# Second-layer sums in two alternating pairs of banks whose idle pair serves attention in fixed steps, and zero products on both row groups

## The chip, the core and the metric

The kernel runs on one core of one Trainium2 chip. The metric is the device time of one execution in microseconds; the time before is 2119.36 us, the median of three runs (2116.33 to 2122.65). Engines are named as in the profile: PE (TensorE matmul), PEld (its weight loads), DVE (VectorE), ACT (ScalarE), POOL (GpSimd) and SP (SyncE, which here issues all DMAs).

## The reference

Agent attention over 4 batches of 12480 tokens with 128 features and 49 agents, then a two-layer network with a squared ReLU, all in fp32:

```python
a2k = sm(agents, k)            # softmax over the 12480 keys, scale 1/sqrt(128)
agent_v = a2k @ v              # 49 x 128 per batch
q2a = sm(q, agents)            # softmax over the 49 agents
x = q2a @ agent_v              # 49920 tokens x 128
h = x @ w_in                   # 128 -> 2048
r = np.maximum(h, 0.0)
out = (r * r) @ w_out          # 2048 -> 128
```

So the work of a batch has an order: all its scores of k, their maximum, the sums over v, and only then can the first layer of its tokens start.

## The kernel before

The 49920 tokens are 52 groups of 960 (13 per batch). For each group, `q_scores` (L291) makes the scores against the agents on PE; `q_shift` (L303, DVE) takes the maximum off; exponent, sum, division and a split into a high and a low fp32r half follow on ACT, DVE and POOL; `q_transpose` (L329, PE) turns the result round, `q_copy` (L337, ACT) brings it to SBUF, and `q_spread` copies it to the other row group by two DMAs. The product `agent_v @ w_in` is folded into one 49 x 2048 matrix per batch (`w_make`, L268), again as high and low halves, so that the first layer is a product with K = 49.

The main loop has 832 steps: group s has 16, i is the step. A step runs `mm1` (L353, six products into one pair of PSUM banks `h`, two row groups side by side), `relu` (L365) and `square` (L369) on ACT, `high` (L373) and `low` (L377) on DVE, and `mm2` (L379, twelve products) for the step that lies LAG = 4 before. Eight steps of `mm2` (j = 0 to 7) add up one output tile of 480 tokens in two banks `out0` and `out1`, one for each row group. `store` (L389) then copies one bank on ACT (L392), adds the other on DVE (L393) and issues the DMA. `mm2` with j = 0 of the next tile starts in the same two banks (L383, L387).

PSUM has eight banks: four for two buffers of `h`, two for `out`, two for `ps_att`, the one pair that serves all attention work in the loop (`bank`, L149). Before the loop, `bank` also hands out `h` buffers.

While the loop runs through one batch, the next batch's attention is woven in: 13 pieces of k (`k_scores`, `k_copy`, `k_pmax`), the maximum over all (`k_max`), 13 pieces of v (`v_hi`, `v_lo`, `k_sub`, `k_exp`, `k_hi`, `k_lo`, `v_acc` L219, `v_sum` L236), `a_final` (L243) and four `w_make`. The order on every engine is written out: each piece of work is put at a time in steps with `at`, and all are sorted by it. `chain` (L412) finds the times: an engine takes at most one piece of attention work per step, a table `hop` gives the least distance from engine to engine, and a range of steps in `banks` keeps a second product out of `ps_att` until the first one's reader has had its step. The products may lie in any step. Work within a step comes as mm1 (i), relu (i + .1), mm2 (i + .2), attention (i + .5), square (.55), high (.6), low (.65).

Before the loop, in the opening, the first batch's attention runs alone: 13 pieces of k scores with one zero product each (`warm_up`, L484: a 64-row product of zeros into `out1`, whose result nobody reads), the maximum, 13 pieces of v (`v_acc_whole`, L227, into `out0`), the weights' conversion from the words as they come (`win_make`, `wo_make` on DVE, L100 to L106), `a_final`, and half of `w_make`. Pieces 0 to 2 of the second batch's k (AHEAD = 3) are scored there too.

Of the kernel before, what the change touches and what calls it, by code (L numbers as in the profile page):

```python
# [9 lines left out]
F32 = mybir.dt.float32  # L10
# [15 lines left out]
def agent_attention_relu2_kernel(ctx: ExitStack, tc: tile.TileContext, qT, kT, v, agT, w_in, w_out, outT):  # L26
# [25 lines left out]
    ew = ctx.enter_context(tc.tile_pool(name="ew", bufs=4))  # L52
    ps_h = ctx.enter_context(tc.tile_pool(name="ps_h", bufs=2, space=bass.MemoryType.PSUM))
    ps_o = ctx.enter_context(tc.tile_pool(name="ps_o", bufs=1, space=bass.MemoryType.PSUM))
    ps_a = ctx.enter_context(tc.tile_pool(name="ps_a", bufs=1, space=bass.MemoryType.PSUM))

    ag_sb = cpool.tile([P, B, 2, A], F32, name="ag_sb")
    nc.sync.dma_start(out=ag_sb, in_=agT)
# [84 lines left out]

    kts, vts, pes, pss = {}, {}, {}, {}

    many = [True]
    turn = [0]

    def bank():  # L149
        turn[0] += 1  # L150
        if many[0] and turn[0] % 3:
            return ps_h.tile([P, 2, 512], F32, name="h")
        return ps_a.tile([P, 2, 512], F32, name="ps_att")

    def piece(n):
        return sk[:, n * G:(n + 1) * G, :]
# [86 lines left out]
    def a_final(step, b):  # L243

        if step == 0:
            if b:
                nc.vector.tensor_tensor(acc[:, 0], acc[:, 0], acc[:, 1], op=ALU.add)
            nc.vector.tensor_tensor(acc[:, 0, :C], acc[:, 0, :C], acc[:, 0, C + 2:], op=ALU.add)
        elif step == 1:
            ps = pss["a"] = bank()[:, 0]  # L250
            nc.tensor.transpose(ps[:, :A2], acc[:, 0, :C], ident[:A2, :A2])
            nc.tensor.matmul(ps[:, P:P + A2], acc[:, 0, C:C + 1].to_broadcast([A2, P]), ident[:A2, :A2], start=True, stop=True)
        elif step == 2:
            t = pss.pop("a")[:, :2 * P].rearrange("p (t x) -> p t x", x=P)
            nc.vector.tensor_copy(av, t[:, :, :A])
            nc.vector.scalar_tensor_tensor(out=av[:, 1], in0=t[:, 1, A:A2], scalar=1e-9, in1=av[:, 1], op0=ALU.add, op1=ALU.add)
            nc.vector.tensor_tensor(av[:, 0], t[:, 0, A:A2], av[:, 0], op=ALU.add)
        else:
            nc.vector.reciprocal(av[:, 1], av[:, 1])
            nc.vector.tensor_tensor(a2[:, :, :A], av[:, 0:1].to_broadcast([P, 2, A]), av[:, 1:2].to_broadcast([P, 2, A]), op=ALU.mult)  # L260

# [3 lines left out]

    W = {}

    def w_make(b, f, step):  # L268
        if f == 0 and step == 0:
            W[b] = (wk.tile([P, NJ, P], F32R, name="w_hi"), wk.tile([P, NJ, P], F32R, name="w_lo"))  # L270
        wh, wl = W[b]
        js = slice(2 * f, 2 * f + 2)
        if step == 0:
            pss["w", f] = bank()[:, 0]
            nc.tensor.matmul(pss["w", f][:AW, :], a2.rearrange("p t a -> p (t a)")[:, :AW], win_sb[:, f * 512:(f + 1) * 512], start=True, stop=True)  # L275
        else:
            ps = pss["w", f].rearrange("p (j e c) -> p j e c", e=2, c=P)
            for e in range(2):
                if step == 1:
                    nc.scalar.copy(wh[ra[e], js], ps[ra[e], :, e])  # L280
                else:
                    nc.vector.tensor_tensor(wl[ra[e], js], ps[ra[e], :, e], wh[ra[e], js].bitcast(F32), op=ALU.subtract)  # L282
# [96 lines left out]
    def mm2(i):  # L379
        t, j = divmod(i, NJ)  # L380
        gh, gl = ghs.pop(i), gls.pop(i)
        if j == 0:
            outs[t] = [ps_o.tile([P, 512], F32, name=f"out{u}") for u in range(2)]  # L383
        todo = [(w, gh, e) for e in range(2) for w in (wo_hi, wo_lo)] + [(wo_hi, gl, e) for e in range(2)]
        for x, (w, g, e) in enumerate(todo):
            for u in range(2):
                nc.tensor.matmul(outs[t][u][:, :TT], w[rg[u], 2 * j + e, :], g[rg[u], e, :], start=j == 0 and x == 0, stop=j == NJ - 1 and x == 5)  # L387
# [7 lines left out]


    LAG = 4
    AHEAD = 3
    steps = []

    def at(t, f, *args):
# [4 lines left out]
    hop = {"PE": {"PE": 1, "ACT": 1, "DVE": 1}, "ACT": {"PE": 2, "ACT": 1, "DVE": 0, "POOL": 0, "SP": 0},  # L406
           "DVE": {"PE": 2, "ACT": 1, "DVE": 1, "POOL": 1, "SP": 0}, "POOL": {"PE": 3, "ACT": 2, "DVE": 2, "POOL": 1}}
    ends = {i for i in range(NG + LAG) if i >= LAG and (i - LAG) % NJ == NJ - 1}
    taken = {(e, i) for i in ends for e in ("ACT", "DVE")}
    banks = set()  # L410

    def chain(t, todo):  # L412

        first = prev = None
        while todo:
            n = 1
            while todo[0][0] == "PE" and n < len(todo) and todo[n][1] in reads_bank and todo[n][0] != "PE":
                n += 1  # L420
            t += hop[prev][todo[0][0]] if prev else 0
            while True:
                g, p, ts = t, None, []
                for e, *_ in todo[:n]:
                    g += hop[p][e] if p else 0
                    while (e, g) in taken:
                        g += 1
                    ts.append(g)
                    p = e
                held = range(ts[0], ts[-1] + 1) if todo[0][0] == "PE" else ()  # L430
                if not banks.intersection(held):
                    break
                t += 1
            banks.update(held)
            for (e, f, *args), g in zip(todo, ts):
                taken.add((e, g))
                at(g + .5, f, *args)
            first = ts[0] if first is None else first
            prev, t, todo = p, ts[-1], todo[n:]
        return first, t  # L440

    reads_bank = (k_copy, k_max, v_sum, a_final, w_make, q_shift, q_copy)

    def plan_tokens(s, base, loaded=False):
        first, end = chain(base, [("PE", q_scores, s), ("DVE", q_shift, s), ("ACT", q_exp, s), ("DVE", q_inverse, s),
                                ("POOL", q_norm, s), ("ACT", q_hi, s), ("POOL", q_lo, s),
                                ("PE", q_transpose, s), ("ACT", q_copy, s)])
        if not loaded:
            at(first - 6, q_load, s)
        at(end + .9, q_spread, s)  # L450
        assert end + 3 < s * NF, (s, end)

    def plan_batch(b, base, span):

        d = (span - 46) / (2 * NS)
        for n in range(NS):
            if b == 1 and n < AHEAD:
                continue
# [2 lines left out]
            if n == NS - 2:  # L461
                chain(end + 1, [("DVE", k_max, 0)])
        _, t0 = chain(end + 1, [("DVE", k_max, 1), ("PE", k_max, 2), ("DVE", k_max, 3), ("PE", k_max, 4), ("DVE", k_max, 5)])
        for n in range(NS):
            t = t0 + 1 + int(n * d)
            first, _ = chain(t - 2, [("ACT", v_hi, n, 0), ("DVE", v_lo, n, 0)])
            _, t2 = chain(t - 1, [("ACT", v_hi, n, 1), ("DVE", v_lo, n, 1)])
            at(first - 6, v_load, b, n)
            _, t1 = chain(t, [("POOL", k_sub, n), ("ACT", k_exp, n), ("ACT", k_hi, n), ("POOL", k_lo, n)])
            _, end = chain(max(t1 + 3, t2 + 2), [("PE", v_acc, n), ("DVE", v_sum, n)])  # L470
        _, end = chain(end + 1, [("DVE", a_final, 0, b), ("PE", a_final, 1, b), ("DVE", a_final, 2, b), ("DVE", a_final, 3, b)])
        for f in range(F // 512):
            _, e = chain(end + 2 + 2 * f, [("PE", w_make, b, f, 0), ("ACT", w_make, b, f, 1), ("DVE", w_make, b, f, 2)])
        assert e + 2 < base + span, (e, base + span)


# [1 line left out]
    warm = wk.tile([P, 512], BF16, name="warm", tag="ob")  # L478
    nc.vector.memset(warm, 0.0)
    nc.vector.memset(acc, 0.0)  # L480
    wps = ps_o.tile([P, 512], F32, name="out1")
    vps = ps_o.tile([P, 512], F32, name="out0")

    def warm_up(n):  # L484
        for _ in range(n):
            nc.tensor.matmul(wps, warm[:L, :P], warm[:L], start=True, stop=True)  # L486

    def begin():
        many[0] = False

    Z, KP = -100.0, 1.9
    at(Z, warm_up, 12)
# [8 lines left out]
        at(Z + x, raw_load, n, src)  # L501
    for n in range(NS):
        t = Z + 6 + KP * n
        at(t, k_scores, 0, n)
        at(t + .1, warm_up, 1)
        at(t + 1.8, k_copy, n)
# [5 lines left out]
    at(t0 - KP + 1.85, k_max, 0)  # L512
    for x in range(1, 6):
        at(t0 + .8 + .4 * x, k_max, x)
    at(t0 + .1, warm_up, 3)
    at(t0 + 1.7, warm_up, 2)
    at(t0 + 2.5, q_scores, 0)
    at(t0 + 4.2, q_shift, 0)
    t0 += 3
# [23 lines left out]
    t += 4.2  # L543
    at(t, v_sum_whole, vps)
    at(t + .2, warm_up, 2)
    for x in range(4):
        at(t + .3 + (0, 1, 2, 2)[x], a_final, x, 0)
    for f in range(2):
        for x in range(3):
            at(t + 4 + .1 * x + .5 * f, w_make, 0, f, x)  # L550
    for n, x in enumerate((t + 1.4, t + 4.6, t + 4.8)):
        at(x, k_scores, 1, n)
        at(x + .01, k_copy, n)
        at(t + 5, k_pmax, n)
    for x in range(7):
        at(t + 5.5 + .1 * x, wo_make, 3, x)
    for x in range(2):
        at(.13 + .01 * x, wo_split, 3, x)
    at(t + 9, begin)
    for f in range(2, F // 512):  # L560
        banks.clear()
        chain(f - 2, [("PE", w_make, 0, f, 0), ("ACT", w_make, 0, f, 1), ("DVE", w_make, 0, f, 2)])
    banks.clear()
    plan_tokens(1, 2, True)
    for s in range(2, NSG):
        plan_tokens(s, (s - 2) * NF + LAG + NJ - 1)
    for b in range(1, B):
        plan_batch(b, (b - 1) * NS * NF, NS * NF)

# [39 lines left out]
```

## Time and profile before

| what | value |
|---|---|
| median of three runs | 2119.36 us (2116.33 to 2122.65) |
| profiled execution, its own time | 2115.72 us |
| its span, first to last instruction | 2113.9 us |
| busy share of the span: PE, PEld, DVE, ACT, POOL | 96%, 89%, 89%, 85%, 12% |
| mean granted clock of TensorE | 0.979 |
| moved by DMA | 129.71 MB, mean 61 GB/s |

How to read the rows: a row of the timeline gives start, length, engine, line, operation, out<-in and shapes, and in brackets how long the engine had been idle before it and what ended that. A row of waits reads "engine line <- who ended the wait: total us, times, longest". Matmul ends are modelled, so a busy PE isn't PE at its peak. The granted clock is that of TensorE, 1.00 being full speed. A span is a little shorter than the time of the execution, and the profiled execution was 3.6 us faster than the median of the runs.

### The profile page before, as it was taken

The page shows a single profiled execution, that of the slowest core. Times are in us where ns is not written, and L with a number is a line of the kernel's source. Part 1 is how long each engine was busy: PE and PEld are TensorE (multiplying, and loading weights), DVE is VectorE, ACT ScalarE, POOL GpSimd, SP SyncE. Part 2 cuts the span into 40 slices and gives each one's busy share as a digit, 9 for nine tenths or more (in the row PEclk, how much of TensorE's full clock was granted, in tenths as well). Part 3 has the DMA queues.
Part 4 walks back from the last instruction along what each step waited for, and adds up shares of the span by engine and source line. Part 5 has one row for each costly group of instructions (what it writes and reads, how often), then busy time and mean ns, then how long its engine had stood idle before and what let it go on. Part 6 is the DMA issues. An engine that isn't in the chain of part 4 may idle for free.

```text
span 2113.9 us, 48363 instructions
## 1 busy us (share of the span) xinstructions
PE 2038.3 (96%) x20056; PEld 1872.4 (89%) x20056; DVE 1884.9 (89%) x2345; ACT 1801.0 (85%) x2234; POOL 248.4 (12%) x199
## 2 busy tenths in 40 slices
PE   9889999999999999999999999999999999999999
PEld 8779988888899999888879999988887899999988
DVE  3678899999899899999989889999989999999997
ACT  1378898888898889888889888888888999999998
POOL 0100002221000001122100000122210000000000
PEclk9989999999999999999999999999999999999999
DMA  6603222222013212223102212213201111111110
GB/s 223 178 22 85 60 56 76 70 55 58 27 51 85 69 52 70 70 55 86 32 27 76 69 60 72 70 50 82 60 27 45 35 48 32 48 32 48 32 39 20
DMA packets 52868, 129.71 MB, mean 61 GB/s; under 512 B 5760, under 2 KB 21248, under 8 KB 52648
## 3 DMA queue, kind: packets, MB, share of 16 engines
q1 hardware_dynamic: 52648, 126.62, 21.0%
q8 instruction: 157, 2.57, 0.5%
q14 instruction: 63, 0.52, 0.1%
HBM read 81.47 MB, written 25.56 MB: 51 GB/s over the span
## 4 chain that ended last, share of the span: by engine, by line
PE 79%; DVE 10%; ACT 6%; issue 5%; DMA 0%; DVEq 0%; SPq 0%; ACTq 0%
PE out L387 45%; PE h L361 22%; PE ps_att L166 6%; DVE gh L373 3%; ACT r L365 2%; DVE gl L377 2%; PE ps_att L225 2%; PE h L166 2%; ACT g L369 2%; DVE ob L393 1%; PE ps_att L335 1%; DVE vs L217 1%; PE ps_att L275 1%; ACT ob L392 0%; PE out L486 0%
## 5 line engine op out<-in xcount | busy, mean ns | idle before, releaser
L377 DVE TENSOR_TENSOR gl<-g,gh 128x960 fp32r<-128x960 f32 x832 | 1020.1, 1226 | 69.6 <-PE out L387 0.9
L365 ACT ACTIVATE r<-h 128x960 f32<-128x960 f32 x832 | 806.4, 969 | 194.0 <-PE h L361 192.1
L387 PE MATMUL out<-gh,wo_hi 64*128 64x480 f32 x3328 | 852.2, 385 | 48.4 <-DVE ob L393 48.4
L369 ACT ACTIVATE g<-r 128x960 f32<-128x960 f32 x832 | 842.2, 1012 | 12.0
L387 PE MATMUL out<-gh,wo_lo 64*128 64x480 f32 x3328 | 841.8, 383 | 0.0
L387 PE MATMUL out<-gl,wo_hi 64*128 64x480 f32 x3328 | 656.7, 383 | 0.0
L387 PEld LDWEIGHTS out<-gh,wo_hi 64*128 64x128 f32 x3328 | 566.0, 187 | 95.4 <-DVE ob L393 67.1
L361 PE MATMUL h<-p_a,w_hi 49*128 49x480 f32 x1664 | 648.2, 391 | 0.0
L373 DVE CAST gh<-g 128x960 fp32r<-128x960 f32 x832 | 580.4, 698 | 37.6 <-ACT g L369 27.9
L387 PEld LDWEIGHTS out<-gh,wo_lo 64*128 64x128 f32 x3328 | 568.7, 189 | 21.1
L361 PE MATMUL h<-p_b,w_hi 49*128 49x480 f32 x1664 | 548.7, 391 | 0.0
L387 PEld LDWEIGHTS out<-gl,wo_hi 64*128 64x128 f32 x3328 | 457.5, 187 | 26.1
L361 PEld LDWEIGHTS h<-p_a,w_hi 49*128 49x128 f32 x1664 | 312.7, 188 | 21.4 <-ACT r L365 4.6
L361 PE MATMUL h<-p_a,w_lo 49*128 49x480 f32 x832 | 316.8, 381 | 0.0
L361 PE MATMUL h<-p_b,w_lo 49*128 49x480 f32 x832 | 316.7, 381 | 0.0
L361 PEld LDWEIGHTS h<-p_b,w_hi 49*128 49x128 f32 x1664 | 303.4, 188 | 11.4 <-DMA p_b<-p_a 0.2
L320 POOL TENSOR_TENSOR e<-e,sm 120x392 f32<-120x392 f32 x52 | 56.5, 1087 | 1245.2 <-DVE sm L317 1143.2
L361 PEld LDWEIGHTS h<-p_b,w_lo 49*128 49x128 f32 x832 | 158.4, 190 | 4.9
L361 PEld LDWEIGHTS h<-p_a,w_lo 49*128 49x128 f32 x832 | 158.4, 190 | 4.5
L166 PEld LDWEIGHTS ps_att<-ag_sb,qt 64*120 64x120 f32 x1632 | 104.5, 184 | 5.9 <-issue 3.3
L166 PE MATMUL ps_att<-ag_sb,qt 64*120 64x49 f32 x1632 | 102.1, 264 | 2.9 <-DVE w_lo L282 2.7
L393 DVE TENSOR_TENSOR ob<-ob,out 128x480 f32<-128x480 f32 x104 | 67.6, 650 | 41.2 <-ACT ob L392 41.0
(96 smaller groups left out, 1374.7 us busy)
## 6 DMA issues: line engine op xcount, KB each, us to landing
vt<-v SPq DMA_DIRECT2D x104, 243.8 KB
kt<-kT SPq DMA_DIRECT2D x52, 480.0 KB
qt<-qT SPq DMA_DIRECT2D x52, 480.0 KB
outT<-ob SPq DMA_DIRECT2D x104, 240.0 KB
p_b<-p_a SPq DMA_DIRECT2D x104, 183.8 KB
raw<-w_in SPq DMA_DIRECT2D x4, 512.0 KB
raw<-w_out SPq DMA_DIRECT2D x4, 512.0 KB
ag_sb<-agT SPq DMA_DIRECT2D x1, 196.0 KB
```

Source lines behind the costliest of these rows:

```text
L166: nc.tensor.matmul(ps[:CH, u, c * A:(c + 1) * A], x[rg[u], h, c, :], ag_sb[rg[u], b, h, :], start=h == 0, stop=h == 1)
L217: eng.tensor_tensor(out=vs[:, :, C + 2:], in0=vts[n][:, halves[h], :C], in1=vs[:, :, :C].bitcast(F32), op=ALU.subtract)
L225: nc.tensor.matmul(pss["v", n][:A2, u, :VW], pe[rc[u], c, :], vs[rc[u], c], start=c == 0, stop=c == G - 1)
L275: nc.tensor.matmul(pss["w", f][:AW, :], a2.rearrange("p t a -> p (t a)")[:, :AW], win_sb[:, f * 512:(f + 1) * 512], start=True, stop=True)
L320: eng.tensor_tensor(out=es[s], in0=es[s], in1=sms.pop(s).to_broadcast([CH, G, A]), op=ALU.mult)
L361: nc.tensor.matmul(h[:, u, :TT], w[ra[u], j, :], PT[s][u ^ lo][ra[u], cs, :], start=x == 0, stop=x == 2)
L365: nc.scalar.activation(rs_[i], hs.pop(i)[:, :, :TT], AF.Relu)
L369: nc.scalar.activation(gs[i], rs_.pop(i), AF.Square)
L373: nc.vector.tensor_copy(ghs[i], gs[i])
L377: nc.vector.tensor_tensor(out=gls[i], in0=gs.pop(i), in1=ghs[i].bitcast(F32), op=ALU.subtract)
L387: nc.tensor.matmul(outs[t][u][:, :TT], w[rg[u], 2 * j + e, :], g[rg[u], e, :], start=j == 0 and x == 0, stop=j == NJ - 1 and x == 5)
L393: nc.vector.tensor_tensor(ob, ob, o[1][:, :TT], op=ALU.add)
```

## The change

- The two `out` banks and the `ps_att` pair become two pairs, `pairs[0]` and `pairs[1]`. Output tile t uses `pairs[t % 2]`; when it starts (j = 0), `use` makes the other pair the one that `bank` hands to attention. In the opening `use(None)` makes it hand out `h` buffers.
- In the loop, attention's products are planned only into `slots`: the steps in which `mm2` has j = 1, 3 or 5. The reader of the result has to lie in the next step at the latest (`ts[-1] <= ts[0] + 1`), otherwise the product goes to a later slot. The set `banks` is gone.
- `w_make` handles two 512-column parts in one product step (both banks of the pair); `a_final` loses its last step, whose work joins the one before it.
- Tokens of group s are planned from step (s - 2) x 16 + 12, before + 11; the pieces of k and v are spread over (208 - 58) / 26 = 5.77 steps, before (208 - 46) / 26 = 6.23. New lower bounds (`free`) keep the split of v behind the v sum that last used its buffer.
- In the opening, `warm_up` issues each zero product twice, once on each row group, into both banks of `pairs[0]`; bank 0 of that pair is also the one that `v_acc_whole` sums into. The scores and `q_shift` of token group 1 move there from the loop. AHEAD is 2, and the second batch's pieces 0 and 1 of k move from the opening to steps 1.5 and 3.5 of the loop; parts 2 and 3 of the first `w_make` stand at steps 0.5 and 2.5.

```diff
-    ps_a = ctx.enter_context(tc.tile_pool(name="ps_a", bufs=1, space=bass.MemoryType.PSUM))
...
-    many = [True]
-    turn = [0]
+    pairs = [ps_o.tile([P, 2, 512], F32, name=f"pair{x}") for x in range(2)]
+    now = [1]
     def bank():
-        turn[0] += 1
-        if many[0] and turn[0] % 3:
+        if now[0] is None:
             return ps_h.tile([P, 2, 512], F32, name="h")
-        return ps_a.tile([P, 2, 512], F32, name="ps_att")
+        return pairs[now[0]]
+
+    def use(x):
+        now[0] = x
...
         if j == 0:
-            outs[t] = [ps_o.tile([P, 512], F32, name=f"out{u}") for u in range(2)]
+            outs[t] = [pairs[t % 2][:, u, :] for u in range(2)]
+            use((t + 1) % 2)
...
-    AHEAD = 3
+    AHEAD = 2
...
+    slots = {i for i in range(LAG, NG) if (i - LAG) % NJ in (1, 3, 5)}
...
-                    while (e, g) in taken:
+                    while (e, g) in taken or (e == "PE" and g not in slots):
                         g += 1
...
-                held = range(ts[0], ts[-1] + 1) if todo[0][0] == "PE" else ()
-                if not banks.intersection(held):
+                if todo[0][0] != "PE" or ts[-1] <= ts[0] + 1:
                     break
...
-        d = (span - 46) / (2 * NS)
+        d = (span - 58) / (2 * NS)
...
     def warm_up(n):
         for _ in range(n):
-            nc.tensor.matmul(wps, warm[:L, :P], warm[:L], start=True, stop=True)
+            for u in range(2):
+                nc.tensor.matmul(pairs[0][:, u, :], warm[rg[u], :P], warm[rg[u]], start=True, stop=True)
...
+    at(t + 1.35, use, None)
+    at(t + 1.4, q_scores, 1)
+    at(t + 5, q_shift, 1)
+    for f, (x, y, u) in enumerate(((t + 4, t + 4.1, None), (t + 4.5, t + 4.6, 1), (.5, .56, 1), (2.5, 2.56, 1))):
+        at(x, use, u)
+        at(x, w_make, 0, (f,), 0)
...
-    for n, x in enumerate((t + 1.4, t + 4.6, t + 4.8)):
+    for n, x in enumerate((1.5, 3.5)):
         at(x, k_scores, 1, n)
-        at(x + .01, k_copy, n)
-        at(t + 5, k_pmax, n)
+        at(x + .06, k_copy, n)
+        at(x + .07, k_pmax, n)
...
-    plan_tokens(1, 2, True)
+    plan_tokens(1, 0)
     for s in range(2, NSG):
-        plan_tokens(s, (s - 2) * NF + LAG + NJ - 1)
+        plan_tokens(s, (s - 2) * NF + NF // 2 + LAG)
```

More of the change, by code (lines that the diff above doesn't have):

```diff
@@ L257, in a_final @@
             nc.vector.tensor_tensor(av[:, 0], t[:, 0, A:A2], av[:, 0], op=ALU.add)
-        else:
             nc.vector.reciprocal(av[:, 1], av[:, 1])
@@ L266, in agent_attention_relu2_kernel, with w_make @@
     W = {}
-    def w_make(b, f, step):
-        if f == 0 and step == 0:
+    def w_make(b, fs, step):
+        if fs[0] == 0 and step == 0:
             W[b] = (wk.tile([P, NJ, P], F32R, name="w_hi"), wk.tile([P, NJ, P], F32R, name="w_lo"))
         wh, wl = W[b]
-        js = slice(2 * f, 2 * f + 2)
         if step == 0:
[L274 to L277, printed above, removed]
+            pss["w"] = bank()
+        for x, f in enumerate(fs):
+            ps = pss["w"][:, x]
+            if step == 0:
+                nc.tensor.matmul(ps[:AW], a2.rearrange("p t a -> p (t a)")[:, :AW], win_sb[:, f * 512:(f + 1) * 512], start=True, stop=True)
+                continue
+            ps = ps.rearrange("p (j e c) -> p j e c", e=2, c=P)
+            js = slice(2 * f, 2 * f + 2)
             for e in range(2):
@@ L408, in agent_attention_relu2_kernel @@
     ends = {i for i in range(NG + LAG) if i >= LAG and (i - LAG) % NJ == NJ - 1}
+    slots = {i for i in range(LAG, NG) if (i - LAG) % NJ in (1, 3, 5)}
     taken = {(e, i) for i in ends for e in ("ACT", "DVE")}
-    banks = set()
     def chain(t, todo):
@@ L429, in chain @@
                     p = e
-                held = range(ts[0], ts[-1] + 1) if todo[0][0] == "PE" else ()
-                if not banks.intersection(held):
+                if todo[0][0] != "PE" or ts[-1] <= ts[0] + 1:
                     break
                 t += 1
-            banks.update(held)
             for (e, f, *args), g in zip(todo, ts):
@@ L442, in agent_attention_relu2_kernel, with plan_tokens @@
     reads_bank = (k_copy, k_max, v_sum, a_final, w_make, q_shift, q_copy)
[L444 to L448, printed above, removed]
+    def plan_tokens(s, base):
+        todo = [("PE", q_scores, s), ("DVE", q_shift, s), ("ACT", q_exp, s), ("DVE", q_inverse, s),
+                ("POOL", q_norm, s), ("ACT", q_hi, s), ("POOL", q_lo, s),
+                ("PE", q_transpose, s), ("ACT", q_copy, s)]
+        first, end = chain(base, todo if s > 1 else todo[2:])
+        if s > 1:
             at(first - 6, q_load, s)
@@ L463, in plan_batch @@
         _, t0 = chain(end + 1, [("DVE", k_max, 1), ("PE", k_max, 2), ("DVE", k_max, 3), ("PE", k_max, 4), ("DVE", k_max, 5)])
+        free = {}
         for n in range(NS):
-            t = t0 + 1 + int(n * d)
-            first, _ = chain(t - 2, [("ACT", v_hi, n, 0), ("DVE", v_lo, n, 0)])
-            _, t2 = chain(t - 1, [("ACT", v_hi, n, 1), ("DVE", v_lo, n, 1)])
+            t, r = t0 + 1 + int(n * d), free.get(n - 2, 0) + 1
+            first, _ = chain(max(t - 2, r), [("ACT", v_hi, n, 0), ("DVE", v_lo, n, 0)])
+            _, t2 = chain(max(t - 1, r), [("ACT", v_hi, n, 1), ("DVE", v_lo, n, 1)])
             at(first - 6, v_load, b, n)
-            _, t1 = chain(t, [("POOL", k_sub, n), ("ACT", k_exp, n), ("ACT", k_hi, n), ("POOL", k_lo, n)])
+            _, t1 = chain(max(t, r - 3), [("POOL", k_sub, n), ("ACT", k_exp, n), ("ACT", k_hi, n), ("POOL", k_lo, n)])
             _, end = chain(max(t1 + 3, t2 + 2), [("PE", v_acc, n), ("DVE", v_sum, n)])
-        _, end = chain(end + 1, [("DVE", a_final, 0, b), ("PE", a_final, 1, b), ("DVE", a_final, 2, b), ("DVE", a_final, 3, b)])
-        for f in range(F // 512):
-            _, e = chain(end + 2 + 2 * f, [("PE", w_make, b, f, 0), ("ACT", w_make, b, f, 1), ("DVE", w_make, b, f, 2)])
+            free[n] = end - 1
+        _, end = chain(end + 1, [("DVE", a_final, 0, b), ("PE", a_final, 1, b), ("DVE", a_final, 2, b)])
+        for f in range(0, F // 512, 2):
+            _, e = chain(end + 2, [("PE", w_make, b, (f, f + 1), 0), ("ACT", w_make, b, (f, f + 1), 1), ("DVE", w_make, b, (f, f + 1), 2)])
         assert e + 2 < base + span, (e, base + span)
@@ L480, in agent_attention_relu2_kernel @@
     nc.vector.memset(acc, 0.0)
-    wps = ps_o.tile([P, 512], F32, name="out1")
-    vps = ps_o.tile([P, 512], F32, name="out0")
+    vps = pairs[0][:, 0, :]
     def warm_up(n):
         for _ in range(n):
-            nc.tensor.matmul(wps, warm[:L, :P], warm[:L], start=True, stop=True)
-    def begin():
-        many[0] = False
+            for u in range(2):
+                nc.tensor.matmul(pairs[0][:, u, :], warm[rg[u], :P], warm[rg[u]], start=True, stop=True)
     Z, KP = -100.0, 1.9
@@ L503, in agent_attention_relu2_kernel @@
         t = Z + 6 + KP * n
+        at(t, use, None if n % 3 else 1)
         at(t, k_scores, 0, n)
@@ L514, in agent_attention_relu2_kernel @@
         at(t0 + .8 + .4 * x, k_max, x)
+    at(t0 + .05, use, 1)
     at(t0 + .1, warm_up, 3)
     at(t0 + 1.7, warm_up, 2)
+    at(t0 + 2.45, use, None)
     at(t0 + 2.5, q_scores, 0)
@@ L545, in agent_attention_relu2_kernel @@
     at(t + .2, warm_up, 2)
[L546 to L550, printed above, removed]
-    for n, x in enumerate((t + 1.4, t + 4.6, t + 4.8)):
+    at(t + .25, use, 1)
+    for x in range(3):
+        at(t + .3 + x, a_final, x, 0)
+    at(t + 1.35, use, None)
[4 more added lines that the diff above has]
+        at(x, w_make, 0, (f,), 0)
+        at(y, w_make, 0, (f,), 1)
+        at(y + .02, w_make, 0, (f,), 2)
+    at(t + 9, use, 1)
+    for n, x in enumerate((1.5, 3.5)):
         at(x, k_scores, 1, n)
-        at(x + .01, k_copy, n)
-        at(t + 5, k_pmax, n)
+        at(x + .06, k_copy, n)
+        at(x + .07, k_pmax, n)
     for x in range(7):
@@ L558, in agent_attention_relu2_kernel @@
         at(.13 + .01 * x, wo_split, 3, x)
[L559 to L563, printed above, removed]
-    plan_tokens(1, 2, True)
+    plan_tokens(1, 0)
     for s in range(2, NSG):
-        plan_tokens(s, (s - 2) * NF + LAG + NJ - 1)
+        plan_tokens(s, (s - 2) * NF + NF // 2 + LAG)
     for b in range(1, B):
```

## The prediction

> **What bounds the kernel now.** I read the page's head, then a table of stretches, then the waits, and last the timeline at single places. The head says that no engine is free enough to be ignored:
>
> ```profile
> span 2113.9 us, 48363 instructions
> PE 2038.3 (96%) x20056; PEld 1872.4 (89%) x20056; DVE 1884.9 (89%) x2345; ACT 1801.0 (85%) x2234; POOL 248.4 (12%) x199
> ```
>
> An average over unlike stages decides nothing, so I cut the span where the attention changes: scores of k against the agents (122 to 315 for the second batch), the v sums (315 to 537), the batch's end with its new first-layer weights (537 to 625), the same v stretch of the last batch (1346 to 1568), and the end of the run, where only tokens are left. Columns: stretch, length, busy us of PE, PEld, DVE, ACT, POOL, granted clock, DMA share, GB/s.
>
> ```profile
> 122.00:315.00 193.00, 192.59 (x2047) 175.30 (x2044) 174.51 (x214) 170.34 (x207) 15.46 (x12) 1.00 0.21 60
> 315.00:537.00 222.00, 206.45 (x1985) 189.98 (x1983) 206.04 (x247) 191.60 (x254) 49.13 (x36) 0.95 0.24 63
> 537.00:625.00 88.00, 86.24 (x807) 75.32 (x805) 79.36 (x108) 79.15 (x97) 5.97 (x5) 1.00 0.16 46
> 1346.00:1568.00 222.00, 206.91 (x1978) 190.64 (x1976) 205.45 (x245) 190.96 (x253) 49.04 (x36) 0.95 0.23 63
> 1657.00:2103.00 446.00, 440.81 (x4268) 410.07 (x4266) 410.82 (x497) 423.80 (x488) 28.74 (x23) 1.00 0.13 38
> ```
>
> While k is scored, PE is busy 192.6 of 193 us: there is nothing to win there. In the v stretch PE is idle 15.6 of 222 us, the clock is 0.95, and DVE is idle only 16.0: two engines of nearly equal need. At the end PE is idle 5.2 of 446 us. The waits (engine, line, for whom; total us, times, longest) name the cause, first for the run, then for 315 to 537, then for 1657 to 2103:
>
> ```profile
> PE out L387 <- DVE ob L393: 48.4, 44, 2.9
> ...
> PE ps_att L225 <- DVE e L301: 7.1, 9, 1.3
> ...
> PE ps_att L225 <- DVE acc L241: 1.4, 3, 0.5
> ```
> ```profile
> PE out L387 <- DVE ob L393: 12.6, 7, 2.9
> ```
> ```profile
> PE out L387 <- DVE ob L393: 5.2, 15, 0.8
> ```
>
> `out` is single: the first product of a new output tile (L387, j = 0) waits until `store` (L392 ACT, L393 DVE) has read the old sums. Of the 48.4 us, three v stretches hold about 3 x 12.6 = 37.8 and the end 5.2. Why the store is late in the v stretch shows in the longest case:
>
> ```profile
> 433.35 0.48 PE L387 MATMUL out<-gh,wo_hi 64*128 64x480 f32 x1
> ...
> 433.81 1.16 DVE L377 TENSOR_TENSOR gl<-g,gh 128x960 fp32r<-128x960 f32 x1
> ...
> 434.89 0.69 DVE L217 TENSOR_TENSOR vs<-vt,vs 120x512 fp32r<-120x512 f32 x1
> ...
> 435.49 0.65 DVE L373 CAST gh<-g 128x960 fp32r<-128x960 f32 x1
> 436.06 0.65 DVE L393 TENSOR_TENSOR ob<-ob,out 128x480 f32<-128x480 f32 x1
> ...
> 436.76 0.77 PE L387 MATMUL out<-gh,wo_hi 64*128 64x480 f32 x1 [2.94 <-DVE ob L393]
> ```
>
> DVE isn't waiting: it works without a break and comes to L393 late, behind gl, the v split and gh. PE waits for a busy DVE. Such a stall costs twice, as the granted clock of the two stretches around it says:
>
> ```profile
> 432.94:436.35 3.41, 0.89 (x6) 0.23 (x3) 3.31 (x6) 3.41 (x6) 0.00 (x0) 1.00 0.00 0
> 436.35:439.76 3.41, 3.00 (x16) 2.50 (x18) 3.38 (x5) 0.56 (x1) 0.00 (x0) 0.50 0.37 119
> ```
>
> After 3.4 us with PE busy for 0.89, the next 3.4 us are granted half the clock.
>
> **The change part by part.** *Two pairs for the sums.* Tile t+1 starts in the other pair, so L387 no longer waits for L393. What inherits the lateness of the store is the first attention product of the next tile, which is fixed at j = 1. That is one whole step behind j = 0; a plain step lasts 1.99 us between these two rows:
>
> ```profile
> 801.38 0.39 PE L361 MATMUL h<-p_a,w_hi 49*128 49x480 f32 x1
> ...
> 803.37 0.39 PE L361 MATMUL h<-p_a,w_hi 49*128 49x480 f32 x1
> ```
>
> From where PE stands today when it stalls, it gets one mm2 (1.3 us, two thirds of a step), a further mm1 and the mm2 of j = 1: about 3.3 us. The longest stall was 2.9, so the store is on time and this wait goes to nothing. What is late next is DVE itself: PE was waiting for work that DVE really had, so the v stretch can shrink only to DVE's need, 206.0 of 222 us. In the stretch 432.94 to 436.35 DVE was busy 3.31 of 3.41, or 97%; as the best density that it can hold I take that: 206.0 / 0.97 = 212.4, a gain of 9.6 us per batch. Bounds: 16.0 (DVE never idle) and 0 (its idle time is made of waits of its own). The half clock is inside these bounds, since DVE's need doesn't depend on it. Three batches: 29 us (0 to 48).
>
> At the end of the run PE may win the whole 5.2; ACT, busy 423.8 of 446, covers that. I take 4 (0 to 5.2). At the batch ends PE idles 1.8 of 88 us; against it the four products of the new weights now come as two lumps of two with their copies and splits in one step each. I take 1 us of gain per batch, 3 in all (-3 to +5).
>
> *Fixed steps.* Attention's PE work may now be issued only in j = 1, 3, 5, and its reader must come in the next step at the latest. A batch has 26 tiles x 3 = 78 such steps and needs 26 for tokens, 26 for k and v, two for the maximum, one for `a_final` and two for the weights: 57. There is room. In the loop no instruction is added or removed; moved are the starts of the k and v work (d falls from 6.23 to 5.77 steps), the last two steps of `a_final`, which now come in one, and with them the loads, on SP alone, whose DMA share of 0.24 leaves cover. Tokens take j = 1 in every tile (base +13 and +21), so a v sum lands mostly in j = 3, two steps behind a product whose reader, for the scores, is DVE. It must wait for that reader, as L225 does today: 7.1 us in nine waits, 0.79 each. Half of 13 v sums per batch, at 0.79 each in place of today's 2.8 per batch: 2 us worse per batch on PE. I charge nothing for it, as DVE's need sets this stretch; without that cover it is 7 us in all, and tile starts behind a v sum in j = 5 (a quarter of 39) would add as much again.
>
> *The opening.* Before the loop the timeline of PE, then DVE, then ACT has:
>
> ```profile
> 47.98 3.66 PE L166 MATMUL h<-ag_sb,kt 64*120 64x49 f32 x31
> ...
> 89.77 1.88 PE L166 MATMUL h<-ag_sb,kt 64*120 64x49 f32 x32 [1.68 <-DMA kt<-kT]
> 91.58 2.05 PE L275 MATMUL h<-win_sb,a 128*113 128x512 f32 x2
> ...
> 95.17 3.56 PE L166 MATMUL h<-ag_sb,kt 64*120 64x49 f32 x64
> ...
> 108.76 2.02 PE L275 MATMUL ps_att<-win_sb,a 128*113 128x512 f32 x2 [7.44 <-DVE w_lo L282]
> ```
> ```profile
> 96.05 0.86 DVE L282 TENSOR_TENSOR w_lo<-ps_att,w_hi 49x256 fp32r<-49x256 f32 x2 [0.75 <-ACT w_hi L280]
> ...
> 100.09 0.43 DVE L100 TENSOR_SCALAR cv_p<-raw 128x512 uint32<-128x512 uint32 x1
> ...
> 118.44 0.57 DVE L296 TENSOR_REDUCE mx<-ps_att 120x8 f32<-120x392 f32 x1 [1.60 <-PE ps_att L166]
> 119.04 0.57 DVE L301 TENSOR_TENSOR e<-ps_att,mx 120x392 f32<-120x392 f32 x1
> ```
> ```profile
> 104.06 0.62 ACT L127 CAST wo_hi<-wo_f 128x512 fp32r<-128x512 f32 x1 [3.60 <-DVE wo_f L106]
> 104.58 1.00 ACT L369 ACTIVATE g<-r 128x960 f32<-128x960 f32 x1
> ```
>
> The first square (104.58) waits behind the cast of the last w_out piece, that one for DVE's conversion that starts at 100.09. Scores of token group 1, whose q was asked for long before, replace those of the second batch's first k piece: the 1.68 us wait goes. DVE gets q_shift (0.57 + 0.57) and loses three maxima of k. So the conversion follows the w_lo that ends at 96.91: 96.91 - 1.68 + 1.14 = 96.4 in place of 100.09, 3.7 us earlier. Two k scores (3.56 together) leave the stretch before the loop and come back in steps 1 and 3, where PE is idle 7.44 us anyway; but all of it now goes through one pair, each product behind the reader of the last, and the third k score stays to be paid. I take 4 us (-4 to +9).
>
> *Zero products on both row groups.* A k piece takes about 3.6 us in the opening (47.98) although the same 32 products take 1.88 at 89.77. The clock has no records before 64; I read the difference as half clock. The dense v products that start at 59.25 change speed within 7 us of it:
>
> ```profile
> 59.25 6.94 PE L231 MATMUL out<-vt,sk 120*49 120x129 f32 x39
> ...
> 65.81 10.30 PE L231 MATMUL out<-vt,sk 120*49 120x129 f32 x91
> ```
>
> (0.18 us each, then 0.11), and these use 120 rows, where the zero products use 64. PE was filled with zero products from 1.19 to 5.87 and that did not raise the speed:
>
> ```profile
> 1.19 4.68 PE out L486 x11
> ```
>
> On both row groups the first twelve probably do; then the k scores themselves (49 columns per load) are too thin to hold it, for even with the doubled zero product of each piece PE streams little. I take one or two 3.4 us stretches at full speed, 2 us of gain. Bounds: 0, and 13 pieces from 3.6 down to 2.3 us (1.88 plus one zero product of 4.68 / 11 = 0.43), 17 us. The doubled products cost nothing where each pair runs side by side, as L361's two row groups do; if not, 32 x 0.43 = 14 us at that same speed, which is the bound on the other side.
> The Trainium skill, "TensorE: Matmul & The Clock Gate", Part 1, says that one busy window of about 3.4 us releases the clock. The row at 1.19 is longer than that and did not; taken at its word, the second row group would change nothing and the sum would be 2 us smaller.
>
> *Sum*: 29 + 4 + 3 + 4 + 2 = 42 us. The profiled execution took 2115.72 us (span 2113.9): 2115.7 - 42 = 2073.7. The three timed runs have their median 3.6 above it, at 2119.36, so I forecast 2077.
>
> **The rivals.** *C, the wait only moves.* DVE's 16 us of idle time in the v stretch are its own (it waits for ACT, and in-order neighbours), and PE, freed at the store, waits at L225 and at tile starts. For it: DVE had work through the whole longest stall. Against it: DVE is idle as much as PE there. Only the end, the opening and a little remain, 12 us: 2107.
>
> *B, the opening runs at full clock throughout.* The first twelve zero products raise the clock and one pair per piece keeps it: 17 in place of 2, so 2062. Against it: the thin scores.
>
> *D, slower: reader waits in the fixed steps.* Without the store as a brake PE runs ahead of DVE, and each v sum in j = 3 stands before everything else on PE until q_shift or the last v sum is read. If DVE is later by the whole step (1.99) that PE runs ahead, and a fifth of it is still to spare, since 27 of 39 v sums wait nothing today, each of the 39 waits 1.6: 62 us against 42 of gain, 2139. It decides from 42 / 39 = 1.1 us per v sum on. For it: today's waits are of just this kind, up to 1.3. Against it: twelve waits in all, 0.7 us on the mean.
>
> *E, the clock falls at every switch of pairs.* If each of 104 tile starts left PE idle long enough for one 3.41 us stretch at 0.50, that is 104 x 1.7 = 177 us: 2119 - 42 + 177 = 2254. Against it: `h` alternates between two pairs in every step, and 122 to 315 has clock 1.00.
> The Trainium skill, the same page, section "A second HAM failure mode: psum-queue depth-cycling", says that cycling through banks can leave PE short idle times that make the clock oscillate; by it the change would be harmful. This trace agrees only where a stall is long.
>
> **How the numbers follow.** Chances: forecast 0.55, B 0.15, C 0.18, D 0.10, E 0.02. A measurement of this kernel can't tell less than 0.3% (6.4 us) from no change. The forecast and B are faster; C, with terms between 2095 and 2118, is faster in about 0.14 of its 0.18; the rest of C and the mild part of D make no change, 0.06; slower keeps 0.10. Faster: 0.84. The forecast's own bounds are 2050 (16 us per v stretch, all of the end, the opening at its best of 9) and 2100. Reaching into B and C, the range is 2047 to 2114; D, E and the edge of C, under 2 in 10, lie outside.
>
> **What would show it.** Right: no wait of L387 for L393; the v stretch some 10 us shorter per batch with DVE above 95%; no granted 0.50 behind tile starts; the k stretch as long as before; the first square near 100. Wrong: L225 or `ps_att`'s successors waiting for L301 or L241 by more than 1.1 us per v sum (D); DVE idle 16 us in the v stretch still (C); k pieces of 2.4 us in the opening (B). The forecast falls if a v stretch, plain steps included, is not shorter, or if the gain stands in the opening alone.

## The result, and the profile after

The changed kernel takes 2045.84 us, the median of four runs (2041.43 to 2059.52), against 2120.26 us before on the same chip: a ratio of 0.9662, 95% interval 0.9614 to 0.971. It is faster by about 74 us, where the prediction had 42; the median lies 1.2 us below the low end of its range, and the interval reaches into it. The profiled execution took 2045.09 us, against 2115.72.

The head of the page after:

```profile
span 2043.3 us, 48393 instructions
PE 1983.5 (97%) x20088; PEld 1855.3 (91%) x20088; DVE 1871.2 (92%) x2345; ACT 1791.7 (88%) x2234; POOL 247.8 (12%) x199
```

Below are the stretches of the changed kernel that run the same steps as those shown of before (k scores, v sums, end of the second batch; v sums of the last batch; end of the run; columns as there):

```profile
97.90:290.00 192.10, 192.10 (x2059) 178.01 (x2057) 171.62 (x210) 168.47 (x203) 12.42 (x10) 1.00 0.21 63
290.00:503.40 213.40, 199.60 (x1990) 191.60 (x1988) 202.88 (x245) 191.87 (x256) 49.52 (x36) 0.98 0.24 66
503.40:589.70 86.30, 86.11 (x828) 75.45 (x825) 80.85 (x109) 78.83 (x97) 5.46 (x4) 1.00 0.16 47
1296.00:1509.80 213.80, 200.33 (x1980) 188.64 (x1980) 203.03 (x245) 191.29 (x255) 49.21 (x36) 0.97 0.24 65
1596.60:2033.00 436.40, 436.40 (x4272) 426.88 (x4270) 408.06 (x499) 417.96 (x488) 30.39 (x24) 1.00 0.14 39
```

The difference of the spans, 70.6 us, divides so (each stretch of before less its like after, all batches). Borders are good to about 1 us. The last row goes from 1657 to 2103.4 before, 0.4 us past the stretch that was shown, where the same step starts as at 2033.0 after:

| stretch | before, us | after, us | gain | forecast |
|---|---|---|---|---|
| opening, up to step 5 | 122.0 | 97.9 | 24.1 | 6 |
| k scores, three batches | 193.0 + 205 + 205 | 192.1 + 203.3 + 203.1 | 4.5 | 0 |
| v sums, three batches | 3 x 222 | 213.4 + 212.8 + 213.8 | 26.0 | 29 |
| batch ends, three | 88 + 89 + 89 | 86.3 + 87.1 + 86.8 | 5.8 | 3 |
| end of the run | 446.4 | 436.4 | 10.0 | 4 |

Waits after, in the v stretch from 290 to 503.4:

```profile
PE pair L226 <- DVE e L304: 6.6, 4, 2.8
PEld pair L391 <- DVE acc L240: 3.9, 1, 3.9
PE pair L391 <- DVE acc L240: 3.5, 1, 3.5
PEld pair L391 <- DVE acc L242: 3.4, 2, 1.7
PE pair L391 <- DVE acc L242: 2.6, 2, 1.3
...
PE pair L167 <- DVE ob L397: 0.6, 1, 0.6
```

The wait of the sums (now L391) for the store (now L397) is gone. What stands in its place is what the prediction named: the v sums (L226) wait for the scores' shift, and a tile start waits for the v sum read from that pair. DVE is busy 202.9 of 213.4 us, 95%. In the end of the run no wait of PE of more than a rounding is left:

```profile
ACT r L368 <- PE h L364: 11.4, 11, 1.1
DVE ob L397 <- ACT ob L396: 9.3, 13, 0.7
```

The opening, PE after (the last row is the k score of step 1.5, which waits 6.42 us until DVE has read the new first-layer weights out of its pair):

```profile
1.19 5.30 PE L491 MATMUL pair<-warm 64*128 64x512 bf16 x24 [1.19 <-DVE warm L484]
6.28 2.00 PE L167 MATMUL pair<-ag_sb,kt 64*120 64x49 f32 x32
...
28.50 1.78 PE L167 MATMUL pair<-ag_sb,kt 64*120 64x49 f32 x32
...
83.53 3.44 PE L167 MATMUL pair<-ag_sb,kt 64*120 64x49 f32 x32 [6.42 <-DVE w_lo L285]
```

All 13 k pieces run at 1.78 to 2.00 us, from 6.28 to 30.3, where before they ended near 51.6: this is the rival B. 24 zero products, two side by side, take 5.30 us; of the twelve on one row group before, the eleven in the profile took 4.68. So the second row group costs next to nothing.

### The profile page after: what moved, and what is told of

Its sections match the earlier page's. It is cut to its first block, busy times and chain, and to the rows that moved or that the text cites. A ratio compares the mean times of both kernels' runs of the same rounds, so it can differ in the third digit from the quotient of the medians.

```text
span 2043.3 us, 48393 instructions
## 1 busy us (share of the span) xinstructions
PE 1983.5 (97%) x20088; PEld 1855.3 (91%) x20088; DVE 1871.2 (92%) x2345; ACT 1791.7 (88%) x2234; POOL 247.8 (12%) x199
## 4 chain that ended last, share of the span: by engine, by line
PE 86%; DVE 8%; issue 4%; ACT 1%; DMA 1%; DVEq 0%; ACTq 0%
PE pair L391 48%; PE h L364 25%; PE pair L167 7%; DVE gh L376 3%; PE pair L338 2%; DVE gl L380 2%; PE pair L226 2%; DVE vs L218 1%; PE h L167 1%; PE pair L232 1%; PE pair L277 1%; DMA vt<-v 1%; PE pair L491 0%; DVE acc L242 0%; ACT r L368 0%
## 5 line engine op out<-in xcount | busy, mean ns | idle before, releaser
L391 PE MATMUL pair<-gh,wo_hi 64*128 64x480 f32 x3328 | 689.5, 382 | 19.5 <-DVE acc L240 10.6
L391 PE MATMUL pair<-gh,wo_lo 64*128 64x480 f32 x3328 | 683.9, 379 | 0.0
L364 PE MATMUL h<-p_b,w_hi 49*128 49x480 f32 x1664 | 645.8, 389 | 0.0
L391 PE MATMUL pair<-gl,wo_hi 64*128 64x480 f32 x3328 | 529.8, 381 | 0.0
L391 PEld LDWEIGHTS pair<-gh,wo_hi 64*128 64x128 f32 x3328 | 368.0, 186 | 41.8 <-DVE acc L240 11.8
L391 PEld LDWEIGHTS pair<-gh,wo_lo 64*128 64x128 f32 x3328 | 370.2, 187 | 18.6
L391 PEld LDWEIGHTS pair<-gl,wo_hi 64*128 64x128 f32 x3328 | 355.4, 185 | 21.7
L364 PEld LDWEIGHTS h<-p_b,w_hi 49*128 49x128 f32 x1664 | 312.2, 188 | 10.6
L167 PEld LDWEIGHTS pair<-ag_sb,qt 64*120 64x120 f32 x1600 | 93.6, 182 | 4.9 <-DVE ob L397 3.1
L397 DVE TENSOR_TENSOR ob<-ob,pair 128x480 f32<-128x480 f32 x104 | 67.6, 650 | 30.4 <-ACT ob L396 30.3
L330 POOL TENSOR_TENSOR pp<-e,pp 120x392 fp32r<-120x392 f32 x52 | 70.9, 1363 | 196.6 <-ACT pp L327 183.5
```

What stands on the lines that cost most here:

```text
L167: nc.tensor.matmul(ps[:CH, u, c * A:(c + 1) * A], x[rg[u], h, c, :], ag_sb[rg[u], b, h, :], start=h == 0, stop=h == 1)
L330: eng.tensor_tensor(out=pps[s][:, :, L:], in0=es.pop(s), in1=pps[s][:, :, :A].bitcast(F32), op=ALU.subtract)
L364: nc.tensor.matmul(h[:, u, :TT], w[ra[u], j, :], PT[s][u ^ lo][ra[u], cs, :], start=x == 0, stop=x == 2)
L397: nc.vector.tensor_tensor(ob, ob, o[1][:, :TT], op=ALU.add)
```

## The experiments

Ratios are to the kernel before on the same chip. The changed kernel, run once more beside the last three, gave 2046.65 us, ratio 0.9647 (0.9621 to 0.9672).

**One row group again.** The changed kernel with

```diff
-            for u in range(2):
+            for u in range(1):
                 nc.tensor.matmul(pairs[0][:, u, :], warm[rg[u], :P], warm[rg[u]], start=True, stop=True)
```

> The changed kernel, but each zero product again on one row group only (the second product of each pair left out). Theory: the second row group is what lifts the clock in the opening, so the 13 k pieces go back from 1.83 us to about 3.5 us each, 13 x 1.7 = 22 us; later work covers a little of it: 18 to 24 us slower than the changed kernel, about 2066. Rival: the moved scores and the freed DMA order made the opening shorter; then the time stays within 5 us of 2046.

2064.79 us, 0.9738 (0.9724 to 0.9753): 19 us slower than the changed kernel by the medians, 16 by the ratios. The k pieces are back at the old pace; two of its rows:

```profile
6.28 3.29 PE L167 MATMUL pair<-ag_sb,kt 64*120 64x49 f32 x30
...
47.98 3.66 PE L167 MATMUL pair<-ag_sb,kt 64*120 64x49 f32 x31
```

In its trace the first relu starts at 94.16 us, 5.3 us earlier than before; in the changed kernel it starts at 75.24, 24.3 earlier. So the moved scores and the freed DVE order are worth 5 us in the opening, and the second row group 19.

**The second row group alone, in the kernel before.**

```diff
-            nc.tensor.matmul(wps, warm[:L, :P], warm[:L], start=True, stop=True)
+            for u, ps in enumerate((vps, wps)):
+                nc.tensor.matmul(ps, warm[rg[u], :P], warm[rg[u]], start=True, stop=True)
```

> The kernel before, with the zero products on both row groups (one into out1 as before, the other into out0) and nothing else. Theory: about 20 us faster than the kernel before, near 2100, with k pieces of 1.8 us. Rival, that the clock needs the new order of the opening as well: within 5 us of 2120.

2101.56 us, 0.992 (0.9892 to 0.9947): 20 us faster, as the first theory had it, with all k pieces fast:

```profile
5.65 1.78 PE L166 MATMUL h<-ag_sb,kt 64*120 64x49 f32 x32
...
28.25 1.81 PE L166 MATMUL h<-ag_sb,kt 64*120 64x49 f32 x32
```

The single times go from 2096.51 to 2114.37; in the profiled execution, at 2104.48 one of the slower ones, the first relu starts 14.7 us earlier than before. The effect needs nothing else of the change.

**Which of the zero products do it.** The changed kernel with both row groups only for the first twelve, `range(2 if n == 12 else 1)`, or only for those between the pieces, `range(1 if n == 12 else 2)`.

> The changed kernel with only the first twelve zero products on both row groups; the later ones, one per k piece, on one group. If the first twelve lift the clock and the scores hold it, the time stays at 2046 (within 4 us). If the pair per piece is needed to hold it, the clock falls after one or two stretches of 3.4 us, and the time goes to about 2063.

> The changed kernel with the first twelve zero products on one row group, and those between the pieces on both. If full activity at the start is needed, k pieces stay at 3.5 us and the time is about 2066. If the pair per piece is enough to lift the clock by itself, a few pieces are slow and the rest fast: 2050 to 2056.

The first gave 2049.37 us (single times 2056.09, 2055.18, 2043.57 and 2041.47), 0.9654 (0.9619 to 0.9689); the second 2062.56 us, 0.9728 (0.9712 to 0.9743). In the trace of the first, k pieces are fast until the granted clock falls from 1.00 to 0.50 at 14.4 us; in that of the second they are slow to the end. First the one, then the other:

```profile
4.16:14.40 10.24, 9.66 (x161) 8.45 (x159) 4.85 (x9) 1.95 (x4) 0.00 (x0) 1.00 0.99 365
14.40:55.30 40.90, 39.79 (x340) 36.61 (x339) 20.88 (x38) 5.96 (x12) 0.00 (x0) 0.50 0.63 206
```
```profile
1.19 4.87 PE L491 MATMUL pair<-warm 64*128 64x512 bf16 x11 [1.19 <-DVE warm L484]
...
6.28 3.08 PE L167 MATMUL pair<-ag_sb,kt 64*120 64x49 f32 x29
...
48.12 3.32 PE L167 MATMUL pair<-ag_sb,kt 64*120 64x49 f32 x31
```

So lifting and holding are two things. Twelve pairs of products, each pair filling both row groups, lift the clock; thin k pieces with a pair of zero products each did not lift it in 45 us, but can hold it once it is up. With one product each the single times, two near 2042 and two near 2056, suggest that they hold it in some executions only; those of the changed kernel, 2041 to 2060, spread as widely, so that a pair per piece holds it better than one product isn't shown. "A few pieces slow, the rest fast" was wrong. Not tested is whether more zero products on one row group, 24 for example, would lift the clock too.

**No alternation.** All output tiles in pair 0, all attention in pair 1, the fixed steps kept:

```diff
-            outs[t] = [pairs[t % 2][:, u, :] for u in range(2)]
-            use((t + 1) % 2)
+            outs[t] = [pairs[0][:, u, :] for u in range(2)]
+            use(1)
```

> The changed kernel with all output tiles in pair 0 and all attention of the loop in pair 1: the fixed steps stay, the alternation goes. Theory: the wait for the store comes back, 46 us slower than the changed kernel (2092), of it about 26 in the v stretches, 10 at the batch ends, 10 at the end of the run. Rival, that the fixed steps and the new spreading gave the gain of the loop: 2046 to 2056.

2138.48 us, 1.0089 (1.0073 to 1.0105): 92 us slower than the changed kernel, twice what was expected, and slower than before in spite of the shorter opening. Its waits over the run, then its stretches of k scores and the end of the run:

```profile
PEld pair L391 <- DVE ob L397: 154.7, 103, 3.2
PE pair L391 <- DVE ob L397: 113.6, 103, 2.8
```
```profile
94.40:296.50 202.10, 194.54 (x2063) 170.62 (x2061) 175.08 (x213) 171.16 (x205) 12.71 (x10) 1.00 0.20 59
1659.20:2122.80 463.60, 443.05 (x4272) 379.20 (x4270) 412.10 (x498) 422.68 (x488) 25.62 (x24) 1.00 0.12 37
```

The store is waited for at all 103 tile starts that follow another tile, 1.1 us each; before it was 44. The kernel before put attention's products into any step, and those that fell on a tile's end gave the store its time. Its trace shows it: at 98 of the 103 tile starts the scores of q (L166) or their transposes (L335) lie between the last product of the old tile and the first of the new one, 49 each. Behind the longer scores PE waits for the store at 6 of 49 starts, behind the shorter transposes at 33 of 49, and at the five starts without either every time. Two such places at the end of the run, first with the scores and no wait, then with a transpose and a wait:

```profile
1680.89 1.76 PE L166 MATMUL ps_att<-ag_sb,qt 64*120 64x49 f32 x29
...
1683.18 0.38 PE L387 MATMUL out<-gh,wo_hi 64*128 64x480 f32 x1
...
1683.40 0.38 PE L387 MATMUL out<-gh,wo_lo 64*128 64x480 f32 x1
```
```profile
1698.34 0.89 PE L335 MATMUL ps_att<-ident_r,pp 64*113 64x64 f32 x13
...
1699.78 0.37 PE L387 MATMUL out<-gh,wo_hi 64*128 64x480 f32 x1
...
1700.47 0.48 PE L387 MATMUL out<-gh,wo_hi 64*128 64x480 f32 x1 [0.29 <-DVE ob L393]
```

The fixed steps never lie there (no tile start of this kernel has such a product ahead of it), so alone they lose that cover. The end of the run, 446.4 us before, takes 463.6. But the loss doesn't lie where it was expected: of the 92 us about 30 are in the k scores, 27 at the end of the run, 21 at the batch ends and only 14 in the v stretches, where 26 were expected. The v stretch of the second batch:

```profile
295.46:515.08 219.62, 202.82 (x2001) 182.60 (x1999) 203.49 (x247) 194.14 (x257) 51.07 (x36) 0.98 0.24 64
```

With 219.6 us, and 219.4 and 218.7 in the other two batches, the v stretches are still shorter than the 222 of before, so in these stretches alone the rival holds for some 10 us: the fixed steps with the new spacing (which of the two, no run separates) are worth that much there, and cost far more elsewhere. The alternation is worth 92 us on the fixed steps; net of what the fixed steps take, the loop gains 46.

**What sets the v stretch.** One kernel leaves half of the products of the v sums out, one half of the split of v on DVE:

```diff
-        for c in range(G):
+        for c in range(H):
             for u in range(2):
                 nc.tensor.matmul(pss["v", n][:A2, u, :VW], ..., stop=c == H - 1)
```
```diff
     def v_lo(n, h, eng=nc.vector):
         vs = vss[n % 2][:, halves[h]]
+        if h == 1 and n > 1:
+            return
```

> The changed kernel with half of the products of each v sum in the loop left out (chunks 4 to 7 of 8), so PE has about 0.5 us less per piece, 39 pieces, 19 us, with DVE and ACT as before. Theory, DVE's need sets the v stretch: the time falls by less than 6 us. Rival, PE and its waits for the readers set it: it falls by 13 to 19 us.

> The changed kernel with the second half of the split of v left out on DVE for pieces 2 to 12 of each batch in the loop: 33 x 0.74 = 24 us less work on DVE in the v stretches, PE as before. Theory, DVE's need sets the v stretch: 14 to 24 us faster than the changed kernel. Rival, PE sets it: less than 6 us faster.

Less PE: 2044.89 us, 0.9657 (0.9623 to 0.969), no difference. Less DVE: 2032.26 us, 0.9587 (0.957 to 0.9605), about 14 us faster. The v stretches of the second and the last batch, first with less PE, then with less DVE:

```profile
289.80:502.80 213.00, 196.65 (x1897) 182.45 (x1895) 203.50 (x244) 191.79 (x256) 48.27 (x36) 0.97 0.24 66
1295.50:1509.60 214.10, 196.85 (x1889) 180.44 (x1888) 204.21 (x244) 191.38 (x255) 48.42 (x36) 0.97 0.24 65
```
```profile
294.30:504.40 210.10, 200.37 (x1989) 192.72 (x1988) 196.95 (x234) 191.48 (x256) 49.86 (x36) 0.97 0.24 67
...
1289.80:1497.40 207.60, 198.68 (x1981) 191.49 (x1980) 195.52 (x234) 190.89 (x255) 51.51 (x36) 0.98 0.25 67
```

The v sums' own busy time on PE falls from 46.6 to 27.6 us over the run, and these 19 us shorten nothing (PE's whole busy time in the two stretches falls by only 3 us each; why not by more stays open). The splits of v on DVE fall from 55.9 to 33.2 us, and these 23 us shorten the stretches by 3 to 6 us each, with DVE at 94%, near the 95% of the changed kernel. DVE's need sets the stretch, though not alone: the gain is at the lower edge of what was expected, and PE's waits for readers are still there.

**Readers earlier.** DVE reads q scores and v sums one place earlier in its order:

```diff
-                at(g + .5, f, *args)
+                at(g - .45 if f in (v_sum, q_shift) else g + .5, f, *args)
```

> The changed kernel, where DVE reads the scores of q and the v sums one place earlier in its order (before high and low of the step of the product, not after). No work is added or removed. If what is left of PE's waits in the v stretch (for the shift at 19.5 us, for the v sums 20 us in the whole run) is only lateness in DVE's order, 15 to 30 us faster, near 2025. If DVE's need sets the stretch, the waits of PE go and come back as waits for gl or for h, and the time stays within 8 us of 2046. Where DVE has room (k stretch, end of the run) it may now wait for PE: up to 0.6 us per product of q, at most 10 us of loss at the end.

2037.90 us, 0.963 (0.9592 to 0.9667): 8 us below the changed kernel and so at the border of the second theory, with an interval that overlaps. In the profiled execution the v stretches are shorter, the k stretches and the end of the run unchanged, and PE's wait for the shift falls from 19.5 us over the run to a third:

```profile
288.10:499.80 211.70, 202.27 (x1988) 187.30 (x1987) 204.23 (x244) 193.74 (x256) 55.28 (x36) 0.98 0.24 66
1290.50:1500.70 210.20, 198.09 (x1980) 181.18 (x1980) 203.26 (x244) 192.89 (x255) 54.49 (x36) 1.00 0.24 66
```
```profile
PE pair L226 <- DVE e L304: 6.6, 8, 1.0
```

That is nearer to the second theory, DVE's need: the waits shrink and the stretch follows by 2 to 4 us only. The loss feared at the end of the run didn't come.

**The spread of the changed kernel, and a better version.** Its single times lie between 2040 and 2060.

> The changed kernel as it is, on the same chip as the three that follow: 2046, with single times between 2041 and 2060. If the spread comes from the clock in the opening, the times near 2060 have a mean clock some 0.01 lower than those near 2045.

> The changed kernel with two pairs of zero products per k piece in place of one. If the spread of the changed kernel (2041 to 2060) comes from a clock that falls back during the k pieces, the extra activity holds it: no time above 2052, and the median at 2046 plus 13 x 0.2 = 3 us at most. Rival, that the spread comes from elsewhere: still single times near 2060, and the median 3 us higher.

> The changed kernel with the conversion of the last w_out piece put ahead of the last v sum of the opening on DVE (where DVE was idle 6.4 us), and its cast ahead of the first relu on ACT. If that conversion is what holds up the first square (80.97, behind the cast at 80.01), the opening ends 4 to 5 us earlier: about 2041. If its words have not landed by then, the v sum waits for them and the time stays at 2046 or grows by up to 4 us.

> The changed kernel with the readers of q scores and v sums one place earlier on DVE, the last conversion earlier, and two pairs of zero products per piece: if the gains add, 2046 - 8 - 4 = 2034, with a spread under 8 us.

The changed kernel again: 2046.65 us (2039.91 to 2053.18). Its profiled execution was the one at 2053.18, and in its k pieces the granted clock goes to 0.50 at 18.46 us:

```profile
15.05 1.81 PE L167 MATMUL h<-ag_sb,kt 64*120 64x49 f32 x32
...
17.47 2.59 PE L167 MATMUL pair<-ag_sb,kt 64*120 64x49 f32 x32 [0.40 <-ACT sk L174]
...
20.22 3.35 PE L167 MATMUL h<-ag_sb,kt 64*120 64x49 f32 x32
```

Ahead of the fall PE had waited 0.40 us for ACT; the kernel with readers earlier waited 0.33 us at the same piece and kept its clock, so what decides stays open. In the first comparison the run at 2059.52 has a mean clock of 0.976, the other three 0.985 to 0.987. With two pairs per piece (`warm_up, 2`): 2045.88 us (2039.24 to 2048.80), 0.9639 (0.9615 to 0.9663); no time above 2052, as expected, but the six runs of the changed kernel beside it reach only 2053.18, so four runs don't show that the extra pair holds the clock. With the last conversion ahead of the opening's last v sum

```diff
-        at(t + 5.5 + .1 * x, wo_make, 3, x)
+        at(t - 1 + .1 * x, wo_make, 3, x)
-        at(.13 + .01 * x, wo_split, 3, x)
+        at(t - .25 + .01 * x, wo_split, 3, x)
```

2039.02 us (2037.81 to 2043.55), 0.9615 (0.9593 to 0.9637): 7.6 us faster on the same chip, more than the 4 to 5 expected, though the intervals overlap, and not by the way that was given: the first relu starts 3.6 us later than in the changed kernel, at 78.80, and the first square at 80.36, hardly earlier than 80.97, but DVE is free afterwards, and step 16 is reached 6 us earlier. All three together: 2034.25 us (2032.40 to 2035.65), 0.9588 (0.9567 to 0.9609), 12 us faster than the changed kernel on that chip, with an interval that is apart from its. In its profiled execution the clock stays up from 3.87 us to 68.7:

```profile
3.87:68.70 64.83, 57.47 (x755) 51.06 (x750) 51.31 (x93) 17.29 (x34) 6.05 (x5) 1.00 0.99 298
```

## Why the prediction was right, and where it was not

*v stretch: right in what sets it, with some luck in the number.* Forecast were 212.4 us per batch from DVE's need of 206.0 at 97%; measured are 213.4, 212.8 and 213.8. DVE's need fell to 203, and its density was 95%: two errors that cancel, since 206.0 at 95% would have been 216.8. The two removals bear out that DVE's need, more than PE's, sets the stretch. The stall's second cost, half clock behind it, shrank too: 0.95 granted became 0.97 to 0.98. The Trainium skill, "TensorE: Matmul & The Clock Gate", section "A second HAM failure mode: psum-queue depth-cycling", describes a kernel whose clock goes up and down because PE idles briefly as it cycles through banks (rival E). The trace disagrees for this alternation: the k stretches and the end of the run, which alternate as well, have 1.00.

*Rivals C and D: fell, but what they named is there.* Over the whole run of the changed kernel L226 waits longer for the shift than the 7.1 us of before:

```profile
PE pair L226 <- DVE e L304: 19.5, 13, 2.8
```

That is 0.5 us per v sum. The tile starts that wait for a v sum's reader (L391 for L240 and L242) add 10.6 and 8.9 us, which makes 1.0 per v sum, just below the 1.1 from which D decides. DVE's need covers most of it: with the readers earlier these waits shrink, and the kernel gains about 8 us.

*End of the run, batch ends and k scores: right in kind, too small.* For the end of the run the step "PE may win the whole 5.2" took the idle time of PE before L387. The weight loads of the same stalls say more, in the kernel before from 1657 to 2103:

```profile
PEld out L387 <- DVE ob L393: 10.9, 15, 1.2
```

Matmul ends are modelled and run into the stall; the gain was 10.0. In the kernel without alternation the same two waits were 20.5 and 30.9 us at the end of the run, and its loss of 27 lies between them. At the batch ends the 5.8 are what PE waited there before (1.8, 2.1 and 1.8 us); I had charged against them for lumps that cost nothing visible. The k scores of the second batch, which I had called full, are within 1 us as long as before; those of the other two batches are some 2 us shorter, though hardly any wait for the store stood there before, and the cause stays open.

*Opening: the moves right, the zero products mis-sized.* The moves gave 5 where I had 4. For the zero products the step that failed is "the k scores themselves are too thin to hold it": 2 us was the term, and 16 to 20 was measured by taking the second row group away and by adding it alone. The bound of 17 was near; rival B was the truth with 0.15 on it. With 20 in place of 2 the forecast would have been about 2059. The Trainium skill's rule in Part 1 of the same page, that one busy window of some 3.4 us releases the clock, holds with both row groups (5.30 us of zero products, and full speed from 6.72 us on) and not with one (4.87 us, then slow). So in this case issuing without a break for that long isn't enough, and what the products fill of the array matters.

*The fixed steps: the step "I charge nothing" hid the larger thing.* I saw them as a cost of waits for readers, 7 us and as much again, where 20 and 19.5 us were measured, and never asked what covered the 59 of 103 tile starts that did not wait before. It was attention's products in the steps at a tile's end; without the alternation, losing that cover costs no less than the change wins in the loop, 46 us.

## What to carry to other kernels

Where a wait shows only at some places, ask what covers the others before moving that work: here the cover was worth as much as the wait. To size a stall of TensorE, read the idle time of its weight loads beside that of its products, whose ends are modelled. And filler products meant to raise the clock should fill both row groups: here that cost next to nothing, while the same products on one row group did not raise it.

## What the runs showed of the hardware

Lifting the granted clock of TensorE and holding it took different activity. At the slow pace, k scores with one zero product or a pair each ran 45 us without a lift (3.3 us or more per piece), although PE was never idle. At full clock the same pieces held it to their end in one execution and lost it after 13.7 us in another of the same program (the two views below), and after 10.2 with one zero product each.

```profile
6.72:34.02 27.30, 25.34 (x456) 23.82 (x454) 21.09 (x36) 6.31 (x13) 0.00 (x0) 1.00 1.02 353
```
```profile
4.80:18.46 13.66, 13.24 (x231) 12.09 (x228) 8.80 (x16) 2.91 (x6) 0.00 (x0) 1.00 1.01 389
18.46:32.00 13.54, 13.54 (x136) 13.37 (x134) 7.92 (x15) 1.94 (x4) 0.00 (x0) 0.50 0.76 268
```

The times of one kernel spread with it by up to 18 us: 2041.43 at a mean granted clock of 0.987, 2059.52 at 0.976. The mean shows it only if the records of the clock reach back to the opening: in the kernel with one row group they begin at 63 us, and its mean of 0.988 is higher than the 0.985 of the changed kernel, which is faster.
